# Loading order at the start, one program order over all engines, and a sixth pair tile in a layernorm, attention and SwiGLU block

## The chip, the cores and the metric

The kernel runs on one core of one Trainium2 chip. The metric is the device time of one execution in microseconds (us); the kernel before was run three times, with 853.94, 855.61 and 853.15 us, so its median is 853.94. A profile is one more execution, with a time and a trace of its own.

## The reference

A transformer block with two residual branches, on 2048 rows of 640 columns in fp32. The attention looks at eight earlier positions, two apart; the feed-forward part is a SwiGLU with 1728 hidden columns.

```python
def _A_ref(x, wqkv, wo):                      # H = 32 heads of Dh = 20
    W, dil = 8, 2
    q, k, v = (x @ wqkv).reshape(B, S, 3, H, Dh).transpose(2, 0, 3, 1, 4)
    idx = pos[:, None] - (arange(W) * dil)[None, :]
    mask = idx >= 0
    logits = einsum("bhsd,bhswd->bhsw", q, k[idx]) * Dh ** -0.5
    attn = softmax(where(mask, logits, -1e9))
    return einsum("bhsw,bhswd->bhsd", attn, v[idx]) @ wo      # heads side by side
def _B_ref(x, w_gate, w_up, w_down):          # F = 1728
    return (silu(x @ w_gate) * (x @ w_up)) @ w_down

h  = x + _A_ref(_layernorm(x), wqkv, wo)
h2 = h + _B_ref(_layernorm(h), w_gate, w_up, w_down)
```

## The kernel before

**Tiling.** The 2048 rows are four blocks of 512 (`NB`), and a block is four rows of 128 partitions (`NJ`; "row j" below means such a group of 128, with 640 columns). The 640 inner columns are five chunks of 128 (`NC`). Every fp32 product is made of three passes over high and low parts: `hi` is the value rounded by ACT's copy to the matmul type fp32r, `lo` the rest, made by a subtraction; the passes are hi by hi, lo by hi and hi by lo. So each operand goes through a cast (ACT, mostly) and a subtraction (DVE, mostly) before PE can use it. `low` at L300 issues that subtraction.

**Stages.** For each block `ln1` (L465) normalises x and puts its transpose into `sha` or `shb`; `qkv` (L528) multiplies it by the weights in four column groups (`NG`, 480, 480, 512 and 448 columns, matmuls at L551) and `evict` (L556 to L558, ACT) takes the results from the banks to a stage, from which they go to scratch in device memory (`ksc`, `vsc`, `qsc`). Attention fetches them from there shifted by the window and works mostly on DVE, in `pq`: the product with the keys (L622) and its sum (L628), the product with the values (L663) and the halving sums (L672), a transpose (L679). `wo` multiplies the result by wo (L756). The feed-forward part `ffn` (L918) goes through 14 tiles of the hidden columns (`NF`; 13 of 128 and a last one of 64). A tile of the ordinary kind is `classic` (L898): `load_ffn` fetches and splits its weights, `proj` (matmuls at L844) makes the gate in bank 5 and the up projection in bank 6, `gate_up` takes the SiLU on ACT (L882), multiplies on DVE (L883, which also frees bank 6) and splits the result (L873, L875, L877), and `down` (L859) adds its share to banks 0 to 4. The low parts of the weights, made in block 0, are kept in device memory in `lsc` and read back (L830) for blocks 1 and 2. All 16 groups of attention work and the feed-forward parts of blocks 0 and 1 run interleaved, DVE on the one while PE is on the other.

**Blocks 2 and 3** share weights in `pair` (L1159). Its first `EARLY` tiles (tiles 0 to 7) are done for block 2 by `classic` and once more for block 3. Tiles 8 to 12 go through `pair_tile` (L966): sums and differences of the two blocks' inputs (`sums`, L931) and of the weights are multiplied by `mult` (L1005, matmuls at L1012), and DVE adds the products together, in the manner of a fast matrix product. It yields the hidden columns of both blocks; block 3's wait in `psc` in device memory until `kept_tile` (L1049) fetches them. `finish` adds the residual (DVE, L1203) and stores.

**The start.** `load_x` (L436, its DMA at L441) fetches row j of block 0 by itself, 320 KB. `load_wqkv` (L504) fetches the first column group in parts of chunks ("fifths", 240 KB each; L515), casts each on ACT (L522) and subtracts on DVE (L523). The first fifth goes out on ACT's DMA queue, all the rest on SP's. `ln1` in block 0 takes rows 0 and 1 with `one_dve` (L360: statistics L367, centring L369) and rows 2 and 3 with `one` (L338: mean and centring on ACT, L345, L346 and L350, and the sum of squares on ACT, L357). A row's five chunks are transposed on PE (L495), four into bank 7 (rows 0, 2) or bank 6 (rows 1, 3) and one into its quarter of bank 5, copied by ACT (L497: the high part) and subtracted by DVE (L498). Before that PE runs ten matmuls on zeros, and an eleventh between rows 0 and 1 (`warm`, L419 to L422). The projection's scaling by 1/sqrt(var) is left to `evict`.

**What sets the order.** Each instruction or small group is an entry of a `Plan` (L133) with its engine, a cost and a priority; `add` finds its dependencies by overlapping memory. `order` (L155) takes from the table `ORDER`, per engine, the sequence of that engine's entries, and makes one program of the five sequences: it goes round the engines and takes from each as many entries as have their dependencies issued. Each engine executes its own entries strictly in that sequence. Where a tile or bank is written by several entries, what a reader waits for also depends on where it stands in the program: it waits for the newest write to that tile that stands ahead of it.

Of the kernel before, what the change touches and what calls it, by code (L numbers as in the profile page):

```python
# [25 lines left out]
EARLY = 8  # L26
# [12 lines left out]
ORDER = {  # L39
# [93 lines left out]
class Plan:  # L133
# [21 lines left out]
    def order(self):  # L155
        mine, queue = {}, {}
        for n, o in enumerate(self.ops):
            mine.setdefault(o[0], []).append(n)
# [34 lines left out]
def program(tc, x_in, wqkv_in, wo_in, ffn_in, ffl_in, const_in, out):  # L193
    nc = tc.nc
    V, A, T, Q, G = nc.vector, nc.scalar, nc.tensor, nc.sync, nc.gpsimd
    P = Plan()
# [5 lines left out]
    with tc.tile_pool(name="sb", bufs=1) as sb, tc.tile_pool(  # L202
# [73 lines left out]
        def f(o, n):  # L276
            return fa[:, o : o + n]
# [1041 lines left out]
```

## Time and profile before

| what | value |
|---|---|
| median of three runs (lowest, highest) | 853.94 us (853.15, 855.61) |
| the profiled execution, its own time | 854.99 us |
| its span, first to last instruction | 853.3 us |
| PE matmul / weight load | 843.5 / 717.0 us busy |
| DVE / ACT / POOL | 689.4 / 418.7 / 3.3 us busy |
| DMA | 177.75 MB, mean 208 GB/s |
| PE's granted clock, mean | 1.0 |

PE is TensorE, PEld its weight loads, which run beside the matmuls; DVE is VectorE, ACT ScalarE, POOL GpSimd, SP SyncE, which issues most DMAs here. L551 is line 551 of the kernel. A group like `L844 PE MATMUL bank<-shb,ra` is all instructions of a line with the same operands; the number in brackets behind a row, or the column "idle before", is the time the engine stood still ahead of it and what it then waited for. DMA rows name the target, the source and the queue that issued it. The engines' busy times overlap, and the share of one says only how much of the span it was at work.

### The profile page before, as it was taken

How to read it: one execution, taken by the hardware profiler on the slowest of the kernel's cores; microseconds unless marked ns; L12 is line 12 of the kernel's file. 1: busy time of each engine (PE TensorE's matmuls, PEld its weight loads, DVE VectorE, ACT ScalarE, POOL GpSimd, SP SyncE). 2: the span in 40 equal slices, each digit the busy share in tenths (PEclk: the TensorE clock that was granted, in tenths of full speed). 3: DMA queues.
4: the chain of work that ended last, by engine and by line, in shares of the span. 5: the costliest groups of instructions: out<-in, count | busy, mean ns of one | idle time of the engine just before them, and what ended most of it. 6: DMA issues, size and time to landing. Idle time of an engine off the chain costs nothing.

```text
span 853.3 us, 10728 instructions
## 1 busy us (share of the span) xinstructions
PE 843.5 (99%) x3977; PEld 717.0 (84%) x3977; DVE 689.4 (81%) x807; ACT 418.7 (49%) x736; POOL 3.3 (0%) x12
## 2 busy tenths in 40 slices
PE   8999999999999999999999999999999999999998
PEld 6888888889988888888887898888888888888886
DVE  5499999999999999989989999997766976452433
ACT  5877385252773435367534458444456333242321
POOL 0000000000000000000000000000000000000000
PEclk9999999999999999999999999999999999999999
DMA  6898797688598898657998986967663233244312
GB/s 218 272 287 203 233 257 196 158 259 213 166 263 277 260 284 268 223 191 229 309 302 243 300 241 224 334 224 276 232 201 93 65 127 87 76 167 142 108 39 84
DMA packets 86852, 177.75 MB, mean 208 GB/s; under 512 B 33408, under 2 KB 51584, under 8 KB 86032
## 3 DMA queue, kind: packets, MB, share of 16 engines
q1 hardware_dynamic: 85248, 176.17, 67.7%
q10 hardware_dynamic: 1552, 0.90, 0.4%
q8 instruction: 31, 0.51, 0.3%
q14 instruction: 21, 0.17, 0.1%
HBM read 132.07 MB, written 43.65 MB: 206 GB/s over the span
## 4 chain that ended last, share of the span: by engine, by line
PE 90%; DMA 5%; DVE 4%; SPq 0%; issue 0%; ACT 0%; DVEq 0%
PE bank L844 30%; PE bank L551 24%; PE bank L859 19%; PE bank L1012 7%; PE bank L756 6%; PE bank L1089 2%; DMA ra<-lsc 2%; DMA fa<-in_ffn_dram 2%; DVE pq L663 1%; PE bank L407 1%; DMA pq<-qsc 1%; DVE pq L672 1%; DVE pq L628 1%; DMA fa<-in_x_dram 0%; DVE h L1203 0%
## 5 line engine op out<-in xcount | busy, mean ns | idle before, releaser
L844 PE MATMUL bank<-shb,ra 128*128 128x512 f32 x1050 | 252.7, 390 | 2.0 <-DVE fa L883 1.2
L844 PEld LDWEIGHTS bank<-shb,ra 128*128 128x128 f32 x1050 | 196.0, 188 | 42.5 <-DVE fa L883 1.7
L859 PE MATMUL bank<-ra,acts 128*128 128x512 f32 x656 | 167.2, 390 | 0.0
L859 PEld LDWEIGHTS bank<-ra,acts 128*128 128x128 f32 x656 | 122.4, 188 | 24.7
L551 PE MATMUL bank<-ra,sha 128*128 128x512 f32 (+2 forms) x480 | 107.5, 381 | 0.6 <-ACT sha L497 0.4
L551 PE MATMUL bank<-ra,shb 128*128 128x512 f32 (+1 forms) x470 | 102.5, 378 | 0.0
L551 PEld LDWEIGHTS bank<-ra,sha 128*128 128x128 f32 x480 | 89.1, 188 | 14.3 <-ACT sha L497 0.6
L551 PEld LDWEIGHTS bank<-ra,shb 128*128 128x128 f32 x470 | 88.1, 188 | 12.9
L622 DVE TENSOR_TENSOR pq<-kv,pq 128x2560 f32<-128x2560 f32 x32 | 90.3, 2822 | 3.6 <-issue 2.1
L663 DVE TENSOR_TENSOR pq<-kv,pq 128x2560 f32<-128x2560 f32 x32 | 90.4, 2824 | 2.3 <-DMA kv<-vsc 1.5
L672 DVE TENSOR_TENSOR pq<-pq 128x1280 f32<-128x1280 f32 (+2 forms) x96 | 89.6, 933 | 2.1
L628 DVE TENSOR_REDUCE pq<-pq 128x128 f32<-128x2560 f32 x32 | 90.1, 2816 | 0.3
L558 ACT ACTIVATE st<-bank,fa 128x480 f32<-128x480 f32 (+3 forms) x120 | 50.8, 472 | 74.2 <-PE bank L551 68.7
L820 DVE TENSOR_TENSOR ra<-fa,ra 128x640 fp32r<-128x640 f32 (+1 forms) x70 | 56.2, 819 | 17.4 <-ACT ra L810 13.5
L825 ACT CAST ra<-fa 128x1280 fp32r<-128x1280 f32 (+1 forms) x41 | 50.2, 1224 | 40.1 <-DMA fa<-in_ffn_dram 24.1
L873 ACT CAST acts<-fa 128x512 fp32r<-128x512 f32 x52 | 32.3, 620 | 70.0 <-DVE fa L883 58.7
L810 ACT CAST ra<-fa 128x640 fp32r<-128x640 f32 x56 | 40.7, 728 | 51.2 <-PE bank L859 44.1
L883 DVE TENSOR_TENSOR fa<-bank,fa 128x512 f32<-128x512 f32 x42 | 28.9, 687 | 40.4 <-PE bank L844 40.2
L882 ACT ACTIVATE fa<-bank 128x512 f32<-128x512 f32 x42 | 25.1, 598 | 68.2 <-PE bank L844 60.7
L756 PE MATMUL bank<-ra 128*128 128x320 f32 x360 | 55.7, 309 | 0.0
L756 PEld LDWEIGHTS bank<-ra 128*128 128x128 f32 x360 | 54.1, 188 | 1.5 <-ACT fa L759 0.3
L859 PE MATMUL bank<-acts,ra 128*128 128x512 f32 x164 | 45.8, 390 | 0.0
(163 smaller groups left out, 872.0 us busy)
## 6 DMA issues: line engine op xcount, KB each, us to landing
fa<-in_ffn_dram SPq DMA_DIRECT2D x47, 960.0 KB, 6.0
kv<-ksc SPq DMA_DIRECT2D x32, 440.0 KB, 6.7
kv<-vsc SPq DMA_DIRECT2D x32, 440.0 KB, 6.9
ra<-lsc SPq DMA_DIRECT2D x21, 640.0 KB, 6.2
lsc<-ra SPq DMA_DIRECT2D x13, 640.0 KB, 4.9
ra<-lsc SPq DMA_DIRECT2D x23, 320.0 KB, 5.0
ksc<-st SPq DMA_DIRECT2D x32, 160.0 KB, 4.4
pq<-qsc SPq DMA_DIRECT2D x16, 320.0 KB, 5.2
```

The costliest lines, as they stand in the source:

```text
L551: T.matmul(banks[bk][:, 0:n], l, r_(wq(g, w, c) + shift, n), start=(p, c) == first_mm, stop=(p, c) == last_mm)
L558: P.add("ACT", act(m) + 0.06, lambda: A.activation(stage_t()[:, o : o + NJ * m].rearrange("p (t j c) -> p t j c", j=NJ, c=w)[:, :, j, :], ...
L622: P.add("DVE", dve(2560), lambda: V.tensor_tensor(pq(PROD, 2560).rearrange("p (j w c) -> p j w c", j=2, w=W), window(ko, 2 * jp), pq(qo + ...
L628: P.add("DVE", dve(2560), lambda: V.tensor_reduce(logits(lo)[:, :, 16 * jp : 16 * jp + 16].rearrange("p h n -> p n h"), pq(PROD, 2560).rea ...
L663: V.tensor_tensor(pq(PROD, 2560).rearrange("p (j n d) -> p j n d", j=2, d=DH), bass.AP(tensor=v.tensor, offset=v.offset, ap=[list(v.ap[0]) ...
L672: V.tensor_add(dst(v), v[:, :, 0:m, :], v[:, :, m : 2 * m, :])
L756: T.matmul(banks[bk][:, 0:320], l, r_(m, 320), start=p == 0 and c == 0, stop=p == 2 and c == NC - 1)
L820: low(640, lambda E, o=o: E.tensor_sub(ws(t, lo + o, 640)[p0:], fa[p0:, raw + o : raw + o + 640], ws(t, hi + o, 640)[p0:].bitcast(F32)), [ ...
L825: P.add("ACT", act(n), lambda: A.copy(ws(wt, gu, n), f(raw, n)), r=[rf(raw, n)], w=[rws(wt, gu, n)], prio=PR["fh"])
L844: T.matmul(banks[bk], ws(wt, gu + 1280 * w + wid * c + col, 128), x(a, c), start=p == 0 and c == 0, stop=p == 2 and c == NC - 1)
L859: T.matmul(banks[k], l, m, start=first and p == 0, stop=stop and p == len(passes) - 1)
L1012: T.matmul(banks[bk], ws(wt, o + 2048 * w + 128 * k, 128), xv_[k](a), start=first and p == 0 and k == 0, stop=stop and p == 2 and k == n - ...
```

## The change

Four things change; no arithmetic outside of them does.

1. `EARLY` falls from 8 to 7: tile 7 of blocks 2 and 3 goes through `pair_tile` and `kept_tile`, so that there are six pair tiles.
2. At the start each fifth of the first weight group is a DMA of its own, and the first one moves from ACT's queue to SP's. The calls now alternate: row 0, fifth 0, row 1, fifths 1 and 2, row 2, fifths 3 and 4, row 3.
3. `ORDER` is one table over all engines, of triples (engine, index, count), and `order` issues the program exactly in that sequence instead of merging five.
4. The table's content is new for every engine. The factors on the planner's bytes for the first transfers (1.45 before) are 1.3, and 1.1 for row 0 of x; `order` does not read them.

```diff
-EARLY = 8
+EARLY = 7
...
-ORDER = {
-    "PE": (
-        0, 2, 1, 3, 5, 4, (10, 6), (25, 2), 16, (27, 5), (6, 2), (32, 2), (17, 6), 34, 23, (35, 7), 24, (42, 8), 8, (50, 3), 9, (53, 15), 70, (68, 2), 73, 72,
...
+    (1, 594, 1), (0, 766, 1), (1, 595, 1), (0, 771, 1), (1, 597, 1), (2, 728, 1), (0, 773, 1), (1, 596, 1), (2, 729, 1), (0, 775, 1), (2, 730, 1), (0, 772, 1),
...
     def order(self):
-        mine, queue = {}, {}
+        mine = {e: [] for e in ENGINES}
         for n, o in enumerate(self.ops):
-            mine.setdefault(o[0], []).append(n)
-        for e, runs in ORDER.items():
-            queue[e] = [mine[e][i] for r in runs for i in (range(r[0], r[0] + r[1]) if isinstance(r, tuple) else (r,))]
-            assert sorted(queue[e]) == mine[e]
-        done, out, at = set(), [], dict.fromkeys(queue, 0)
-        while len(out) < len(self.ops):
-            before = len(out)
-            for e, q in queue.items():
-                while at[e] < len(q) and self.ops[q[at[e]]][3] <= done:
-                    done.add(q[at[e]])
-                    out.append(q[at[e]])
-                    at[e] += 1
-            assert len(out) > before
+            mine[o[0]].append(n)
+        out, done = [], set()
+        for e, i, c in ORDER:
+            for n in mine[ENGINES[e]][i : i + c]:
+                assert self.ops[n][3] <= done
+                done.add(n)
+                out.append(n)
+        assert len(done) == len(self.ops)
         return out
...
-                P.add("SP", 0.45, lambda j=j: Q.dma_start(f(XR + 640 * j, 640), x_in[0, :, j, :]), w=[rf(XR + 640 * j, 640)], prio=0, nbytes=1.45 * nb(128, 2560))
+                P.add("SP", 0.45, lambda j=j: Q.dma_start(f(XR + 640 * j, 640), x_in[0, :, j, :]), w=[rf(XR + 640 * j, 640)], prio=0, nbytes=(1.3 if j else 1.1) * nb(128, 2560))
...
-                    first = g == 0 and ks[0] == 0
-                    P.add("ACT" if first else "SP", 0.45, lambda: (A if first else Q).dma_start(f(o, n).rearrange("p (k c) -> p k c", c=m)[:, :, o0:o1], wqkv_in[h, :, ks[0] : ks[-1] + 1, lo : lo + o1 - o0]),
+                    P.add("SP", 0.45, lambda: Q.dma_start(f(o, n).rearrange("p (k c) -> p k c", c=m)[:, :, o0:o1], wqkv_in[h, :, ks[0] : ks[-1] + 1, lo : lo + o1 - o0]),
...
         load_wqkv(0, ((0,),))
-        load_wqkv(0, ((1, 2),))
         load_x(0, (1,))
-        load_wqkv(0, ((3, 4),))
-        load_x(0, (2, 3))
+        load_wqkv(0, ((1,), (2,)))
+        load_x(0, (2,))
+        load_wqkv(0, ((3,), (4,)))
+        load_x(0, (3,))
```

The calls set the numbering of the entries; the sequence on SP is the table's. All line numbers rise by 117 or 118: L441 becomes L559, L497 becomes L615, L551 becomes L668, L844 becomes L961, L883 becomes L1000, L1012 becomes L1129.

SP's sequence at the start, before. A row gives the line, what it does, the tile written and read (`fa` is the fp32 work tile, `in_x_dram` and `in_wqkv_dram` the inputs) and its shape; x2 stands for two in a row. A transfer of 128x480 is one fifth, of 128x960 two.

```order
L441 DMA fa_65<-in_x_dram 128x640 x2
L515 DMA fa_65<-in_wqkv_dram 128x960
L441 DMA fa_65<-in_x_dram 128x640
L515 DMA fa_65<-in_wqkv_dram 128x960 x2
L441 DMA fa_65<-in_x_dram 128x640
L515 DMA fa_65<-in_wqkv_dram 128x960
```

The rows are 0 and 1, then 2, then 3; the third transfer of weights is already one of the second column group. The same place in the changed kernel:

```order
L559 DMA fa_65<-in_x_dram 128x640 x3
L632 DMA fa_65<-in_wqkv_dram 128x480 x3
L559 DMA fa_65<-in_x_dram 128x640
L632 DMA fa_65<-in_wqkv_dram 128x480 x2
L632 DMA fa_65<-in_wqkv_dram 128x960 x2
L632 DMA fa_65<-in_wqkv_dram 128x480
L556 DMA fa_65<-in_x_dram 128x2560
```

The first three are now rows 0, 2 and 1, ahead of any weight; the five fifths follow, row 3 among them, and then the second group; block 1 of x (L556) comes before the third.

ACT's sequence at the start, before (`sha` takes the transposed rows' high parts, `ra` the weights' high parts):

```order
L515 DMA fa_65<-in_wqkv_dram 128x480
L310 ACT_TABLE_LOAD
L310 ACTIVATE fa_65<-fa_65 128x1
L522 CAST ra_66<-fa_65 128x480
L497 CAST sha_131<-bank5_74 128x128
L497 CAST sha_131<-bank7_76 128x512
L497 CAST sha_131<-bank5_74 128x128
L522 CAST ra_66<-fa_65 128x480 x2
L497 CAST sha_131<-bank6_75 128x512
L345 ACTIVATE fa_65<-fa_65 128x640
L346 ACTIVATE fa_65<-fa_65 128x1
L350 ACTIVATE fa_65<-fa_65 128x640
```

and after:

```order
L428 ACT_TABLE_LOAD
L428 ACTIVATE fa_65<-fa_65 128x1
L463 ACTIVATE fa_65<-fa_65 128x640
L464 ACTIVATE fa_65<-fa_65 128x1
L468 ACTIVATE fa_65<-fa_65 128x640
L615 CAST sha_129<-bank7_76 128x512
L475 ACTIVATE fa_65<-fa_65 128x640
L639 CAST ra_66<-fa_65 128x480 x2
L615 CAST sha_129<-bank6_75 128x512
L615 CAST sha_129<-bank7_76 128x512
L639 CAST ra_66<-fa_65 128x480
```

Row 2's centring (L463, L464, L468) now stands first, then the copy of row 0 from bank 7, row 2's squares (L475), two fifths, and the copies of rows 1 and 2 from banks 6 and 7. In the program ahead of the copy from bank 7 stand only row 0's transposes.

In the middle of the program the place on DVE of the multiplication that frees bank 6 is shown by a stretch of block 0's feed-forward part, before (L663 and L672 are attention, L820 the low parts of weights, L883 the multiplication, L875 the low part of its result):

```order
L663 TENSOR_TENSOR pq_87<-kv_68,pq_87 128x2560
L820 TENSOR_TENSOR ra_66<-fa_65,ra_66 128x640 x2
L883 TENSOR_TENSOR fa_65<-bank6_75,fa_65 128x512
L672 TENSOR_TENSOR pq_87<-pq_87 128x2x640
L875 TENSOR_TENSOR acts_2056<-fa_65,acts_2056 128x512
L672 TENSOR_TENSOR pq_87<-pq_87 128x2x320
L672 TENSOR_TENSOR pq_87<-pq_87 128x2x160
L679 STREAM_TRANSPOSE pq_87<-pq_87 128x2x5x32
```

and after:

```order
L780 TENSOR_TENSOR pq_88<-kv_68,pq_88 128x2560
L1000 TENSOR_TENSOR fa_65<-bank6_75,fa_65 128x512
L937 TENSOR_TENSOR ra_66<-fa_65,ra_66 128x640 x2
L992 TENSOR_TENSOR acts_2087<-fa_65,acts_2087 128x512
L789 TENSOR_TENSOR pq_88<-pq_88 128x2x640
L937 TENSOR_TENSOR ra_66<-fa_65,ra_66 128x640
L789 TENSOR_TENSOR pq_88<-pq_88 128x2x320
L789 TENSOR_TENSOR pq_88<-pq_88 128x2x160
L796 STREAM_TRANSPOSE pq_88<-pq_88 128x2x5x32
```

Here L1000 now stands right behind the multiply of 2560 columns, ahead of the two weight subtractions that it followed before. Over the whole program 9 of the 42 such operations stood right behind one of 2560 columns before, and 14 of 41 do after.

More of the change, by code (lines that the diff above doesn't have):

```diff
@@ L36 @@
 PR = {'x': 0.4, 'wqd': 10, 'wqh': 10, 'wql': 10, 'qev': 6, 'kvs': 6, 'atl': 10, 'exp': 2.2, 'ost': 1, 'wod': 6, 'woh': 8, 'wol': 0.5, 'old': 6, 'fld': 4, 'lst': 10, 'wev': 3, 'fh': 1.2, 'fl': 0.4, 'ln1': 10, 't1': 1.5, 'wo0': 4, 'wo': 6}
-ORDER = {
[24 rows of a table removed]
-    ),
-    "ACT": (
[19 rows of a table removed]
-    ),
-    "DVE": (
[20 rows of a table removed]
-    ),
-    "POOL": (
-        (0, 17), 34, (17, 6), 35, (23, 11), (36, 3),
-    ),
[18 rows of a table removed]
-    ),
-}
+ENGINES = ("PE", "ACT", "DVE", "POOL", "SP")
+ORDER = (
[212 rows of a table added]
+)
 class Plan:
@@ L513, in ld @@
                 def ld(h, o0, o1, lo, ks=ks, o=o, n=n):
-                    first = g == 0 and ks[0] == 0
-                    P.add("ACT" if first else "SP", 0.45, lambda: (A if first else Q).dma_start(f(o, n).rearrange("p (k c) -> p k c", c=m)[:, :, o0:o1], wqkv_in[h, :, ks[0] : ks[-1] + 1, lo : lo + o1 - o0]),
-                          w=[rf(o + m * i + o0, o1 - o0) for i in range(len(ks))], prio=PR["wqd"] * (g > 0), nbytes=nb(128 * len(ks), 4 * (o1 - o0)) * (1.0 if g else 1.45))
+                    P.add("SP", 0.45, lambda: Q.dma_start(f(o, n).rearrange("p (k c) -> p k c", c=m)[:, :, o0:o1], wqkv_in[h, :, ks[0] : ks[-1] + 1, lo : lo + o1 - o0]),
+                          w=[rf(o + m * i + o0, o1 - o0) for i in range(len(ks))], prio=PR["wqd"] * (g > 0), nbytes=nb(128 * len(ks), 4 * (o1 - o0)) * (1.0 if g else 1.3))
                 ld(g, 0, min(m, 480), c0)
```

290 rows, old and new, of the table ORDER are left out of this document.

## The prediction

> **What bounds the kernel now.** I began with the first part of the page and the sum over its chain of waits.
>
> ```profile
> span 853.3 us, 10728 instructions
> PE 843.5 (99%) x3977; PEld 717.0 (84%) x3977; DVE 689.4 (81%) x807; ACT 418.7 (49%) x736; POOL 3.3 (0%) x12
> ```
>
> PE is busy for 843.5 of 853.3 us, so 9.8 us are idle. A table of stretches shows where they lie (the first columns are the stretch, its length, then busy time and count of PE, PEld, DVE, ACT, POOL).
>
> ```profile
> 0.00:10.00 10.00, 6.18 (x22) 4.26 (x22) 5.27 (x12) 3.31 (x7) 1.18 (x7) 1.00 0.81 294
> 400.00:500.00 100.00, 98.05 (x454) 81.81 (x453) 93.31 (x88) 42.86 (x62) 0.00 (x0) 1.00 0.97 289
> 660.00:745.00 85.00, 85.00 (x377) 70.38 (x376) 58.36 (x87) 28.50 (x44) 1.36 (x3) 1.00 0.27 89
> 840.00:853.30 13.30, 9.46 (x44) 7.49 (x42) 4.88 (x8) 1.32 (x3) 0.00 (x0) 1.00 0.25 99
> ```
>
> The first ten microseconds hold 3.8 us of idle PE, the end 3.8, the stage from 400 to 500 some 1.95; the pair stage (660 to 745) none. The waits of PE name who was late in the first three that count.
>
> ```profile
> PE bank L495 <- DVE fa L369: 2.0, 2, 1.5
> PE bank L422 <- POOL ra L1220: 1.4, 1, 1.4
> PE bank L844 <- DVE fa L883: 1.2, 1, 1.2
> PE bank L844 <- DMA ra<-lsc: 0.7, 1, 0.7
> ```
>
> So a change pays here in three ways only: fewer matmuls, useful matmuls sooner at the start, or fewer stalls in the middle. ACT and DVE have room of their own and count only where PE waits for them.
>
> **The sixth pair tile.** Tile 7 of the feed-forward part leaves the ordinary scheme, in which blocks 2 and 3 take 2 projections of 3 passes over 5 chunks each, 60 matmuls of 512 columns, and enters `pair_tile`, whose calls of `mult` make 7 x 6 + 4 x 3 = 54. The chain of waits has a long unbroken piece of that line.
>
> ```profile
> 661.62 14.28 PE bank L1012 x63
> ```
>
> That is 0.2267 us each, and six fewer save 6 x 0.2267 = 1.36 us of PE. The tile's extra sums and differences fall on DVE and ACT and its intermediate goes out to `psc` and back. The stretch from 660 to 745 above has five such tiles with DVE busy 58.4 of 85 us, ACT 28.5 and the DMA share at 0.27, and no idle PE; a sixth of the same density hides as well. If that cover were gone, each operation would cost its length, but a third of DVE's time is free, so I count nothing.
>
> **The start.** These rows of the timeline carry it (start, length, engine, line, operation, and in brackets the idle time before it).
>
> ```profile
> 0.81 0.86 SPq L441 DMA_DIRECT2D fa<-in_x_dram  x2
> 0.81 0.41 ACTq L515 DMA_DIRECT2D fa<-in_wqkv_dram  x1
> 5.00 0.89 DVE L367 BATCH_NORM_STATS2 fa<-fa 128x6 f32<-128x320 f32 x2 [2.86 <-DMA fa<-in_x_dram]
> 6.17 0.55 DVE L369 TENSOR_SCALAR fa<-fa 128x640 f32<-128x640 f32 x1
> 6.87 0.74 PE L495 MATMUL bank<-fa 128*128 128x128 f32 x5 [1.46 <-DVE fa L369]
> 7.80 0.55 DVE L369 TENSOR_SCALAR fa<-fa 128x640 f32<-128x640 f32 x1
> 8.40 0.77 PE L495 MATMUL bank<-fa 128*128 128x128 f32 x5 [0.56 <-DVE fa L369]
> 8.77 0.92 ACT L497 CAST sha<-bank 128x128 fp32r<-128x128 f32 x3 [3.01 <-PE bank L495]
> 9.57 0.49 PE L551 MATMUL bank<-ra,sha 128*128 128x480 f32 x1 [0.41 <-ACT sha L497]
> 10.55 0.61 ACT L497 CAST sha<-bank 128x512 fp32r<-128x512 f32 x1
> 11.03 0.77 ACT L345 ACTIVATE fa<-fa 128x640 f32<-128x640 f32 x1
> 12.89 1.07 ACT L522 CAST ra<-fa 128x480 fp32r<-128x480 f32 x2
> 22.12 0.75 ACT L357 ACTIVATE fa<-fa 128x640 f32<-128x640 f32 x1
> 22.85 0.73 ACT L357 ACTIVATE fa<-fa 128x640 f32<-128x640 f32 x1
> ```
>
> Row 0 of x is there at 5.0 us. Its four transposes end near 7.5, yet ACT's first copy of it starts only at 8.77, right after the second group of transposes at 8.40 began: the copy from bank 5 stands first in ACT's order and waits for the newest write to that bank, which is row 1's. So rows 0 and 1 both have to be through before one matmul of the projection runs, at 9.57. Two parts of the change act here. The row of x no longer shares the DMA engines with the first fifth of the weights, and the new program order lets ACT copy row 0's wide part when row 0's own transposes are done.
>
> When does row 0 land? The answers of the DMA view, first for the transfers of 0.81 us, then for one that ran alone at 10.90, and the rate in steps of half a microsecond from zero:
>
> ```profile
> fa<-in_x_dram SPq DMA_DIRECT2D x1, 320.0 KB, 4.2
> fa<-in_wqkv_dram ACTq DMA_DIRECT2D x1, 240.0 KB, 4.3
> fa<-in_wqkv_dram SPq DMA_DIRECT2D x1, 480.0 KB, 3.5
> GB/s 0 0 0 46 79 163 250 393 423 416 417 415 410 420 425 422 415 422 392 382 169 5 0 61 131 215 401 222 104 215 245 56 0 0 54 84 73 326 392 158
> ```
>
> The late bound is no gain: 0.81 + 4.2 = 5.0. The early bound takes the lone transfer: 3.5 us for 480 KB, less 160 KB at about 417 GB/s (0.4), is 3.1, so 3.9. Without the 246 thousand bytes of weights beside it, at the rate of these rows, row 0 would be 0.59 sooner, at 4.4. I take 4.5, since most of the wait is the slow climb of the rate, which the change leaves. The Trainium skill ("DMA: Bandwidth & Descriptors", section "Queues, rings and completion order") says that each DMA engine takes turns between the queues that have work; by that rule half of the turns go back to row 0 and the gain is the whole 0.59, the sum below 0.1 better. The trace agrees so far: 320 KB on one queue and 240 KB on the other landed 0.1 us apart.
>
> On SP the order is now rows 0, 2, 1, three single fifths, row 3, two fifths. At 417 GB/s a row takes 0.79 us and a fifth 0.59, so row 2 lands at 5.3, row 1 at 6.1, the first fifth at 6.7 (before: 5.1), the last near 9.9. From there ACT alone sets the pace. By the rows above, centring a row takes it 11.03 to 12.89 = 1.86 us, the sum of squares 22.12 to 22.85 = 0.73, a copy of 512 columns 0.48 until the next may start and 0.61 until done, a fifth 0.5 and 0.57. In its new order: row 2 centred 5.3 to 7.2; row 0 copied 7.2 (its transposes end near 6.9: 4.5 + 1.72 on DVE + 0.7); squares 7.7 to 8.4; first fifth done 9.0; second 9.5; row 1 copied by 10.0; row 2 by 10.5; third fifth by 11.0; row 3 centred 10.9 to 12.8; fourth fifth by 13.3. The first matmul can start at about 9.1, behind row 2's transposes. Now the matmuls, against these pieces of the chain:
>
> ```profile
> 10.23 3.12 PE bank L551 x13
> 13.35 0.55 PE bank L495 x5
> 13.90 5.62 PE bank L551 x26
> 19.96 0.65 PE bank L551 x3
> 20.73 16.73 PE bank L551 x77
> ```
>
> Before, at 20.73 us all 20 transposes and 1 + 13 + 26 + 3 = 43 matmuls were done, and from there PE never waits. A matmul takes 5.62 / 26 = 0.216. After: nine of the first 18 are done when the third fifth is there at 11.0, nine more take 1.95 (13.0), row 3's transposes 0.55 (13.6), and 25 more 5.4, so the same point is reached at 19.0, 1.7 us sooner. With row 0 at 5.0 it is 1.2, at 3.9 it is 2.3, if DVE's and ACT's copies keep up as in the rows; a slip of half a microsecond in that chain brings the low end to 0.7. I take 1.6. The first fifth of the weights costs nothing by being 1.6 us later, since ACT reaches it at 8.4; the splitting adds two issues on SP at 0.43 (0.86 / 2 above), under transfers already queued.
>
> **The middle and the end.** All queues have new orders. The two stalls of the middle (1.24 and 0.71) come from places that move: DVE's L883, which frees the bank for the up projection, stood behind a multiply of 2560 columns, and a stored weight landed late. The groups of the page give that multiply's length.
>
> ```profile
> L663 DVE TENSOR_TENSOR pq<-kv,pq 128x2560 f32<-128x2560 f32 x32 | 90.4, 2824 | 2.3 <-DMA kv<-vsc 1.5
> ```
>
> By the order, 9 of the 42 such operations before stand right behind one of DVE's 2560-wide operations, and 14 of 41 after. At one stall of 1.24 in nine that is 0.7 us more; the two old stalls may go (1.95 less) or recur. I take the middle as unchanged, with 1.95 less and 1.5 more as the ends of the likely case. The mask and the halo rows are loaded later, block 1 of x earlier, behind a PE that has 77 matmuls queued: nothing. The end keeps its form (last matmul, one DVE sum, one store): nothing.
>
> Sum: 1.36 + 1.6 = 2.96 us. The profiled execution took 854.99 us with a span of 853.3; the median of the runs is 853.94, 1.05 below it. Taken off the median: 851.0 us.
>
> **The rivals.** A measurement of this kernel can tell about 0.3% from no change, that is 2.56 us: below 851.4 is faster, above 856.5 slower.
>
> The middle improves too: both stalls go, 851.0 - 1.95 = 849.1. For it speaks that every queue is ordered anew; against it, that more of the bank-freeing operations stand behind long ones.
>
> The start gives nothing: ACT now does a row's centring and squares (1.86 + 0.73) ahead of its first weight, and if row 0 lands at 5.0 and the copies slip by another microsecond, the first matmul is at 10.6 instead of 9.57, made up by the third row's transposes being done; only the pair tile is left, 853.94 - 1.36 = 852.6. This is also the case in which the change doesn't do what its words say: by the order three rows go ahead of the weights, not one.
>
> PE's clock falls back at the start. The ten warming matmuls took 4.02 us where ten at 0.2267 take 2.27:
>
> ```profile
> 1.39 4.02 PE L422 MATMUL bank<-ra 128*128 128x512 f32 x10 [1.39 <-POOL ra L1220]
> ```
>
> If PE dropped to that again at its gaps after 5.4 us, another 1.75 would be lost: 852.8. Against it: before, gaps of 1.46, 0.56 and 0.41 were followed by 13 matmuls at 0.24 each, and the new gaps are shorter (0.9, then under half a microsecond). The Trainium skill ("TensorE: Matmul & The Clock Gate", section "Part 1: The HAM clock gate (the "warmup" mystery)") has the rule: an idle window of about 3.4 us halves the clock, and the window runs freely. By it a sparse start can be caught; the trace has no such case, its granted clock is 1.00 in every stretch.
>
> Slower than before: DVE becomes the wait in the middle, where the stretch from 400 to 500 us above has it busy 93.3 of 100. PE's next up projection waits for L1000 (L883 before), and L1000 for the 2.82 us ahead of it. At the 1.24 us of the one stall seen, five of the fourteen places give 6.2, 857.2 us; it decides from an extra loss of 5.5. Against it: eight of the nine places before cost nothing, since a down projection covers them.
>
> **How the numbers follow.** The forecast has 0.55; both stalls gone 0.13; an empty start 0.18; the clock 0.05; DVE in the middle 0.09. Of the forecast's case, whose own spread is about 1 us either way round 851.0, seven parts in ten lie below 851.4: 0.55 x 0.7 + 0.13 = 0.51 faster; 0.165 + 0.18 + 0.05 = 0.40 the same; 0.09 slower. The range runs from the case without stalls, 849.0, to the empty start with 1 us more of stalls, 853.6; left out are the slow case and about 1 in 10 beyond the ends.
>
> **What would show it.** Right: DVE's first statistics start near 4.5, ACT's first copy near 7.2, PE's first projection matmul near 9.1, and 43 of them with all transposes done by 19.0; six matmuls fewer; PE idle in the first ten microseconds still near 3 us, in the middle about 2. Wrong: row 0 at 5.0, a first matmul after 9.6, matmuls at 0.4 us behind 9 us, or PE's waits for L1000 over 4 us in total.

## The result

The changed kernel takes 850.97 us (median of 20 runs, 849.79 to 854.62). The kernel before, run in turn with it, takes 855.6 (20 runs, 852.82 to 860.1). The ratio is 0.9946, 95% interval 0.9931 to 0.9961: faster, by 4.6 us, half a per cent. The time was forecast at 851.0 and came out there. The drop was forecast at 2.96, from a median of three runs (853.94) that lay below that of twenty. So two things need explaining: 4.6 us instead of 3, and why the kernel before spreads over 7 us.

The profiled execution of the changed kernel took 850.46 us. The first part of its page:

```profile
span 848.7 us, 10718 instructions
PE 841.7 (99%) x3971; PEld 716.4 (84%) x3971; DVE 694.1 (82%) x815; ACT 420.7 (50%) x738; POOL 2.6 (0%) x11
```

Six matmuls fewer, as counted. PE is idle for 7.0 us instead of 9.8. The stretches that lost time before:

```profile
0.00:10.00 10.00, 7.02 (x28) 5.47 (x29) 5.66 (x13) 6.36 (x13) 1.16 (x7) 1.00 0.81 277
400.00:500.00 100.00, 100.00 (x462) 83.87 (x461) 96.40 (x89) 44.09 (x62) 0.00 (x0) 1.00 0.97 299
840.00:848.70 8.70, 4.85 (x24) 3.68 (x22) 3.43 (x6) 0.00 (x0) 0.00 (x0) 1.00 0.39 151
```

The end is unchanged (3.85 idle). The stretch from 400 to 500, which lost 1.95, loses nothing, although DVE is busier there (96.4 of 100). PE's waits confirm it. All that the view names, with their total, count and longest:

```profile
PE bank L613 <- DVE fa L487: 1.6, 1, 1.6
PE bank L540 <- POOL ra L1337: 1.4, 1, 1.4
```

No L1000 and no stored weights (`lsc`) are left. The start, in rows of the timeline:

```profile
3.86 0.89 DVE L485 BATCH_NORM_STATS2 fa<-fa 128x6 f32<-128x320 f32 x2 [1.74 <-DMA fa<-in_x_dram]
4.62 0.74 ACT L463 ACTIVATE fa<-fa 128x640 f32<-128x640 f32 x1 [2.33 <-DMA fa<-in_x_dram]
6.53 0.59 ACT L615 CAST sha<-bank 128x512 fp32r<-128x512 f32 x1
6.77 0.89 DVE L485 BATCH_NORM_STATS2 fa<-fa 128x6 f32<-128x320 f32 x2 [1.19 <-DMA fa<-in_x_dram]
8.54 1.25 PE L613 MATMUL bank<-fa 128*128 128x128 f32 x9 [1.60 <-DVE fa L487]
9.56 4.16 PE L668 MATMUL bank<-ra,sha 128*128 128x480 f32 x18
```

Row 0 is there at 3.9 us (before 5.0) and ACT copies it at 6.5 (before 8.8). Yet the first projection matmul stands at 9.56, as before: row 1 went out third, landed at 6.7, and its transposes stand ahead of that matmul. What is gained shows behind it. Two pieces of the chain of waits:

```profile
9.80 3.91 PE bank L668 x18
13.71 0.55 PE bank L613 x5
14.26 18.72 PE bank L668 x87
```

At 14.26 all transposes and 18 matmuls are done, and from there a matmul takes 18.72 / 87 = 0.215. The 43rd is through at 14.26 + 25 x 0.215 = 19.6, before at 20.73: 1.1 us. For the two profiled executions that makes 1.36 (pair tile) + 1.1 (start) + 1.95 (waits of the middle) = 4.4 of the 4.6 between the spans.

### The profile page after: what moved, and what is told of

It is laid out like the page before. It is cut to its first block, busy times and chain, and to the rows that moved or that the text cites. A ratio compares the mean times of both kernels' runs of the same rounds, so it can differ in the third digit from the quotient of the medians.

```text
span 848.7 us, 10718 instructions
## 1 busy us (share of the span) xinstructions
PE 841.7 (99%) x3971; PEld 716.4 (84%) x3971; DVE 694.1 (82%) x815; ACT 420.7 (50%) x738; POOL 2.6 (0%) x11
## 4 chain that ended last, share of the span: by engine, by line
PE 97%; DVE 1%; DMA 1%; ACTq 0%; issue 0%; SPq 0%; ACT 0%
PE bank L961 33%; PE bank L668 24%; PE bank L976 22%; PE bank L1129 9%; PE bank L873 6%; PE bank L1206 2%; PE bank L525 1%; DMA fa<-in_x_dram 1%; ACTq L1272 0%; PE bank L613 0%; PE bank L1313 0%; DVE fa L1246 0%; DVE fa L485 0%; SPq L559 0%; DVE fa L1260 0%
## 5 line engine op out<-in xcount | busy, mean ns | idle before, releaser
L961 PE MATMUL bank<-shb,ra 128*128 128x512 f32 x1035 | 248.0, 390 | 0.1
L961 PEld LDWEIGHTS bank<-shb,ra 128*128 128x128 f32 x1035 | 193.1, 188 | 39.7 <-ACT fa L999 0.9
L668 PE MATMUL bank<-ra,sha 128*128 128x512 f32 (+2 forms) x480 | 105.6, 379 | 0.0
L668 PE MATMUL bank<-ra,shb 128*128 128x512 f32 (+1 forms) x470 | 102.6, 378 | 0.0
L668 PEld LDWEIGHTS bank<-ra,sha 128*128 128x128 f32 x480 | 89.5, 188 | 12.8
L668 PEld LDWEIGHTS bank<-ra,shb 128*128 128x128 f32 x470 | 88.0, 188 | 12.6
L937 DVE TENSOR_TENSOR ra<-fa,ra 128x640 fp32r<-128x640 f32 x69 | 55.0, 819 | 17.1 <-ACT ra L927 15.3
L1000 DVE TENSOR_TENSOR fa<-bank,fa 128x512 f32<-128x512 f32 x40 | 27.5, 688 | 43.4 <-PE bank L961 29.4
```

What stands on the lines that cost most here:

```text
L668: T.matmul(banks[bk][:, 0:n], l, r_(wq(g, w, c) + shift, n), start=(p, c) == first_mm, stop=(p, c) == last_mm)
L937: low(640, lambda E, o=o: E.tensor_sub(ws(t, lo + o, 640)[p0:], fa[p0:, raw + o : raw + o + 640], ws(t, hi + o, 640)[p0:].bitcast(F32)), [ ...
L961: T.matmul(banks[bk], ws(wt, gu + 1280 * w + wid * c + col, 128), x(a, c), start=p == 0 and c == 0, stop=p == 2 and c == NC - 1)
```

## The experiments

Every kernel below computes the whole reference. Names with b are edits of the kernel before, with a of the changed one. Each has one trace, that of its first run. "Row 0" is the start of DVE's first statistics there, when row 0 of x has landed (5.00 us in the kernel before, 3.86 in the changed one); the "48th" is the start of the 48th projection matmul, with all transposes and nothing but the start ahead of it (21.45 before, 20.40 after).

| run | n | lowest, median, highest us | ratio to before, interval | row 0 | 48th |
|---|---|---|---|---|---|
| b_two_moves | 12 | 852.31, 852.82, 854.80 | 0.9960 (0.9939 to 0.9980) | 4.63 | 21.05 |
| b_lsc | 12 | 852.49, 853.34, 855.51 | 0.9979 (0.9965 to 0.9993) | 4.70 | 21.13 |
| b_copy2 | 12 | 851.81, 852.21, 854.26 | 0.9958 (0.9935 to 0.9980) | 5.09 | 21.59 |
| b_start | 12 | 850.52, 853.61, 858.24 | 0.9969 (0.9945 to 0.9992) | 3.94 | 19.88 |
| b_start2 | 12 | 850.51, 851.23, 855.06 | 0.9955 (0.9929 to 0.9981) | 3.76 | 19.88 |
| a_pair5 | 12 | 851.46, 853.44, 857.07 | 0.9966 (0.9943 to 0.9989) | 3.89 | 20.08 |
| a_merge | 12 | 850.56, 852.19, 857.39 | 0.9963 (0.9939 to 0.9988) | 3.80 | 20.46 |
| a_late | 12 | 851.08, 855.47, 863.49 | 0.9999 (0.9972 to 1.0025) | 3.77 | 19.58 |
| a_lsc | 6 | 849.59, 849.85, 850.22 | 0.9939 (0.9920 to 0.9958) | 3.82 | 19.74 |
| a_rows | 12 | 851.22, 853.74, 857.00 | 0.9979 (0.9962 to 0.9996) | 4.05 | 20.77 |
| a_w0_act2 | 12 | 850.34, 850.77, 851.69 | 0.9939 (0.9912 to 0.9966) | 5.00 | 20.60 |
| a_best | 12 | 849.57, 849.91, 851.63 | 0.9923 (0.9899 to 0.9948) | 3.88 | 19.74 |

The kernel before, beside them on three chips, had medians of 855.31, 856.54 and 856.13, from 852.2 to 862.4. That spread makes the intervals wide, so most of what follows compares kernels whose own runs lie close together; their medians come from different chips and are not paired. The chips themselves differ little: the lowest run of the kernel before is 852.20, 852.29 and 852.20 on them. The ratios in the table are those on record; they are not quotients of these medians.

The 99 runs of the kernel before on these chips fall into two groups by the mean granted clock that is on record for each. In 48 it is 0.998 or less, and their median is 857.5 us; in 51 it is 0.999 or 1.000, and their median is 853.9. Every run above 857.7 is of the first group. A stretch of 3.4 us at half clock, as b_start below has one, lowers the mean to 0.998. So in about half of its runs PE's clock seems to fall once or more.

**b_two_moves.** The two stalls of the middle, undone where they stood.

```diff
+MOVES = (("DVE", 496, 282), ("SP", 429, 280))
 ORDER = {
...
+            for w, i, j in MOVES:
+                if w == e:
+                    queue[e].remove(mine[e][i])
+                    queue[e].insert(queue[e].index(mine[e][j]), mine[e][i])
             assert sorted(queue[e]) == mine[e]
```

> The kernel before, with two entries moved in its table: on DVE the multiplication of block 1's tile 5 that frees bank 6 (L883) goes ahead of the 2560-column multiply it stood behind, and on SP the load of tile 8's stored low weights goes ahead of one load of values for the attention. Theory A (the gain after is a sum of three: start 1.0, sixth pair tile 1.4, the two stalls in the middle some 2.0 us): PE's waits for L883 (1.24) and for the stored weights (0.71) are gone, nothing takes their place, and the time falls by 2.0 to 2.5 us, to a ratio of 0.9971 to 0.9977. Theory B (these stalls are chance of one execution, or PE just waits a little later): a ratio within 0.001 of 1.

Both waits are gone, the median is 2.5 us under the 855.31 beside it, and the highest of 12 runs is 854.8 where before went to 862.4. Theory A was right on the places; that the spread goes too spoke for B's word "chance". The load of the stored weights, on SP's queue, in the trace of before and then of this run:

```profile
471.93 0.43 SPq L830 DMA_DIRECT2D ra<-lsc  x1
```

```profile
469.14 0.32 SPq L835 DMA_DIRECT2D ra<-lsc  x1
```

The view of the tile `lsc` for that one load gives its landing, with the same numbers in both:

```profile
DMA to landing us min/median/max: 11.6/11.6/11.6
```

In before PE wanted it at 482.9 (0.71 ahead of 483.62): 11.0 us after the issue. Any delay is a stall. The moved load lands at 469.14 + 11.6 = 480.7, and PE comes to it near 480.8, five matmuls behind 479.75, so it has almost no room either; b_copy2, with the same move, waits for it in its trace:

```profile
PE bank L849 <- DMA ra<-lsc: 0.3, 1, 0.3
```

**b_start.** The changed kernel's code with eight ordinary tiles, its order up to the 44th projection matmul, before's from there.

```diff
-EARLY = 7
+EARLY = 8
```

> The kernel before with the changed kernel's start alone: its transfers and its sequences on all engines up to the 44th matmul of the projection, then everything in the order of before, with eight ordinary tiles. Theory A: the first projection matmul at 9.6 us, the 48th at 20.4 instead of 21.4, both stalls of the middle still there, and the time 1.0 us lower, a ratio near 0.9988. Rival, the start's 1.6 us as forecast: a ratio near 0.9981. Theory B (the gain at the start shifts transfers against DVE and is lost in the middle): 1.000, with other or longer stalls.

The start came out as theory A had it or better (48th at 19.9). The ratio, 0.9969, cannot tell 1.0 from 1.6 us here, for the middle is before's, and in this profiled execution it was bad. PE's rows around tile 8, then two of its four waits:

```profile
480.02 1.29 PE L928 MATMUL bank<-shb,ra 128*128 128x512 f32 x5
485.24 5.14 PE L928 MATMUL bank<-shb,ra 128*128 128x512 f32 x15 [3.92 <-DMA ra<-lsc]
```

```profile
PE bank L928 <- DMA ra<-lsc: 3.9, 1, 3.9
PE bank L928 <- DVE fa L967: 1.2, 1, 1.2
```

The same load, issued at 471.21, was used at 485.24, 14.0 us later. And the wait cost more than itself. Stretches of half a microsecond; the first 1.00 or 0.50 behind POOL's column is the granted clock:

```profile
484.50:485.00 0.50, 0.00 (x0) 0.00 (x0) 0.00 (x0) 0.00 (x0) 0.00 (x0) 0.94 1.14 283
485.00:485.50 0.50, 0.26 (x1) 0.26 (x2) 0.00 (x0) 0.00 (x0) 0.00 (x0) 0.50 1.15 272
487.50:488.00 0.50, 0.50 (x3) 0.36 (x2) 0.19 (x1) 0.22 (x1) 0.00 (x0) 0.50 1.00 391
488.50:489.00 0.50, 0.50 (x4) 0.41 (x3) 0.50 (x1) 0.00 (x0) 0.00 (x0) 1.00 0.98 400
```

PE's clock fell to half at the end of a gap of 3.92 us and stayed there until near 488.4 (the slice from 488.0 has 0.64), with two or three matmuls begun in a slice instead of four. PE worked from 485.24, so some 3.1 us went at half speed, about 1.6 us lost by estimate. The Trainium skill ("TensorE: Matmul & The Clock Gate", section "Part 1: The HAM clock gate (the "warmup" mystery)") has it: an idle window of about 3.4 us halves the clock, and it comes back after a busy one. The trace agrees, with 3.92 idle and some 3.4 at half. In a_late below, gaps of 2.56 and 0.93 left it at 1.00. The mean clock of this run is 0.998. That the slower half of the runs of the kernel before had such a gap as well is likely but not shown, since there is no trace of them.

**b_lsc.** SP's move alone.

```diff
-MOVES = (("DVE", 496, 282), ("SP", 429, 280))
+MOVES = (("SP", 429, 280),)
```

> The kernel before with one entry moved on SP alone: tile 8's stored low weights of block 1 are loaded ahead of the attention's values instead of behind them, some 2.8 us earlier; the multiplication L883 stays behind the 2560-column multiply. Theory D (the kernel before varies from 852 to 862 us because this load lands about when PE wants it, and a long wait also drops PE's clock): the runs lie close together, within some 3 us, as with both moves (852.3 to 854.8), their median is about 1.2 us above that of both moves, near 854.0, and PE waits for L883 alone. Theory E (DVE's multiplication is the cause of the spread): the runs spread as before, over 6 us or more.

The runs lie within 3.0 us (852.49 to 855.51, where the kernel before went from 852.29 to 859.44 beside them), as theory D said, so this load is most of what spread them. The median is 0.5, not 1.2, above that of both moves. In its profiled execution PE did not wait for L883's counterpart: DVE began the multiply ahead of it at 458.0 instead of 460.5. In the kernel before DVE had stood still earlier (2.1 us for nothing that the profile shows, 0.8 for keys), and here it had not. So L883's stall, 1.24 us in before and 1.2 in b_start, is a matter of chance as well.

**a_lsc.** The same idea on the changed kernel: SP's entries 414 (tile 3's low weights), 423 (tile 6) and 432 (tile 8) some places earlier.

```diff
 SP:
-... 258, 257, 419, 414 ... 265, 266, 270, 264, 423 ... 283, 432 ...
+... 414, 258, 257, 419 ... 423, 265, 266, 270, 264 ... 432, 283 ...
```

> The changed kernel with three loads of stored low weights in block 1 (tiles 3, 6 and 8) a few places earlier on SP, ahead of the attention loads and stores they stood behind. Theory D: the changed kernel too has runs in which such a load is late (849.8 to 854.6 in 20 runs); with more room the runs lie within 2 us and the median falls by 0.5 to 1 us, to about 850.2, a ratio to before of 0.994. Rival (the spread of the changed kernel has another cause, or the attention loads that are pushed back now make DVE late): median 851 or more, spread 4 us or more.

All 6 runs lie within 0.63 us, at 849.85: the rival is out, and no other version spreads less or has a lower median. Two later kernels with the same three moves lie within 1.35 us (a_w0_act2) and 2.06 us (a_best) in 12 runs. PE waits only at the start:

```profile
PE bank L543 <- POOL ra L1340: 1.4, 1, 1.4
PE bank L616 <- DVE fa L490: 1.0, 1, 1.0
```

**a_late.** Tile 8's load late on SP.

```diff
 SP:
-... 283, 432, 433, 437, 284, 435, 401, 400, 399, 436 ...
+... 283, 433, 437, 284, 435, 401, 400, 399, 432, 436 ...
```

> The changed kernel with the same load (tile 8's stored low weights, block 1) issued some 9 us later on SP, behind a load of values and three loads of attention results; nothing else moves. Theory D: PE waits there 4 to 5 us for it, the granted clock falls behind the wait for about 3 us, which costs another 1.5, and every run rises by 5 to 7 us, to 856 to 858, above the kernel before. Without a fall of the clock the rise is the wait alone, 4 to 5 us. Rival (the load is early enough in the changed kernel, with 13 us from issue to need, that the delay is absorbed by the transfers around it): under 2 us.

The median rose by 4.5 us over 850.97, but not by the way expected: the lowest run is 851.08, the highest 863.49. In the profiled execution the late load cost 0.93; two other waits cost more. The rows of the loads, and the third wait:

```profile
423.69 1.43 PE L964 MATMUL bank<-shb,ra 128*128 128x512 f32 x5 [2.56 <-DMA ra<-lsc]
489.94 1.42 PE L964 MATMUL bank<-shb,ra 128*128 128x512 f32 x5 [0.93 <-DMA ra<-lsc]
```

```profile
PE bank L671 <- ACT st L678: 2.1, 1, 2.1
```

The first is tile 3's load, which this kernel issues as the changed one does. The last stands at 69.38 us: a load of x, issued at 48.18, landed 15.1 us later (10.8 in the changed kernel), ACT stood still 4.92 us for it, and the copy that PE waited for came behind. So another load than those of the stored weights can be late too; a_rows has the same wait of PE with 1.4 us, and a_best moves this load. The load made late went out at 484.74, 13.6 us later than in the changed kernel, and landed in 5.2; in the changed kernel it took 7.3. So theory D's sum, a fixed stall of 4 to 5 us, was wrong. The profiled execution kept its clock at 1.00. Seven of the other 11 runs have a mean clock of 0.994 to 0.998, the longest (863.49) 0.994; where they waited is not known, as there is no trace of them.

**a_merge.** The changed kernel's sequences through before's merge in `order`.

```diff
-        for e, i, c in ORDER:
-            for n in mine[ENGINES[e]][i : i + c]:
-                assert self.ops[n][3] <= done
-                done.add(n)
-                out.append(n)
+        queue = {e: [] for e in ENGINES}
+        for e, i, c in ORDER:
+            queue[ENGINES[e]] += mine[ENGINES[e]][i : i + c]
+        done, out, at = set(), [], dict.fromkeys(queue, 0)
...
```

> The changed kernel with the same sequence on each engine, but merged into one program engine by engine as before, instead of in the order of the one table. Theory A (what counts is each engine's own sequence): the same time as the changed kernel, a ratio to before of 0.9946, within 0.001. Theory C (the one program order is what removes waits, since a reader waits for the newest write to a tile that stands ahead of it in the program): waits like the one of ACT's first copy come back, at the start and in the feed-forward part, and the time rises by 0.5 us or more.

Open. The median is 1.2 above the changed kernel's, but the intervals of the two ratios overlap. Its trace has one wait that the changed kernel lacks, and once more tile 3's load:

```profile
14.02 0.33 PE L618 MATMUL bank<-fa 128*128 128x128 f32 x1 [0.59 <-DVE sha L621]
419.46 1.43 PE L966 MATMUL bank<-shb,ra 128*128 128x512 f32 x5 [0.17 <-DMA ra<-lsc]
```

The 0.59 is of theory C's kind: a transpose into a quarter of bank 5 waits for DVE's subtraction (L621), by our reading because it reads other quarters and now stands ahead of it in the program. So the one order is worth at most 0.6 us at the start, and the 48th shows none of it (20.46, against 20.40 in the changed kernel); more is not shown.

**a_pair5.** The changed kernel with one pair tile less.

```diff
-EARLY = 7
+EARLY = 8
```

> The changed kernel with five pair tiles instead of six: its order up to tile 7 of block 2, then the sequence of before, shifted, with a few entries around the seam moved. Theory A: six more matmuls of 0.2267 us, so 1.36 us over the changed kernel if the seam costs nothing, a ratio to before near 0.996; PE's waits tell what the seam adds (each of its microseconds is to be taken off). Rival (the sixth pair tile also costs something on DVE, so that leaving it out gives part of it back): less than 1 us over the changed kernel.

Its lowest run is 1.67 above the changed kernel's lowest. In the profiled execution the seam, where the two orders meet, costs 0.50:

```profile
631.83 1.43 PE L963 MATMUL bank<-shb,ra 128*128 128x512 f32 x5 [0.50 <-DVE fa L1002]
```

The profiled spans differ by 1.5 (850.2 and 848.7). Without the 0.50, and with the 0.32 by which this start came sooner (48th at 20.08 and 20.40), 1.3 is left for the pair tile, near 1.36; the medians (853.44 against 850.97) are blurred by the loads in the middle.

**b_start2.** b_start with both moves of the middle; in its numbering of SP's entries the load is 432.

```diff
-... DVE 282, 496 ... SP 283, 432 ...
+... DVE 496, 282 ... SP 432, 283 ...
```

> The kernel before with both moves of the middle (L883 ahead of the long multiply, tile 8's stored weights earlier) and the changed kernel's start; eight ordinary tiles. Both moves alone gave 852.8 us with little spread. Theory A with the start at the size that the traces show (the 48th projection matmul at 20.0 us on average, before 21.2): 1.2 us less, 851.6, within 0.4. The forecast's term: 1.6 less, 851.2. What is left from here to the changed kernel with its loads moved (849.85) is then the pair tile, 1.36 by the count.

851.23: 1.59 below b_two_moves, and a_lsc is 1.38 below this. Those are near the two terms of the forecast, 1.6 and 1.36, but theory A's 851.6 within 0.4 holds this median as well. By lowest runs the steps are 1.80 and 0.92, and by the 48th this start gains 1.2 (21.05 to 19.88). Neither step is pure: this kernel also has the one program order throughout, and a_lsc another order in the middle. The only wait of PE that the view names is that for the zeros of the warming:

```profile
PE bank L507 <- POOL ra L1304: 1.4, 1, 1.4
```

**b_copy2.** Both moves, and the copy from bank 7 ahead of that from bank 5.

```diff
-MOVES = (("DVE", 496, 282), ("SP", 429, 280))
+MOVES = (("DVE", 496, 282), ("SP", 429, 280), ("ACT", 7, 8))
```

> The kernel before with both moves of the middle and ACT's copy of row 0 from bank 7 ahead of its copy from bank 5; nothing else of the start changes. Theory A (the wait for row 1 by ACT's first copy costs something at the start): that copy starts near 7.3 us instead of 8.8, the first projection matmul behind row 1's transposes near 9.2, and the time falls by 0.2 to 0.5 us from 852.8. Rival (PE has to pass row 1's transposes anyway, so the copy's wait is covered): the same time within 0.1, and the wait of PE for that copy (0.4) replaced by one for weights.

0.61 below b_two_moves in the median, 0.50 in the lowest. The trace doesn't show how: in its execution row 0 landed late (5.09), and the copy, behind row 0's transposes, started at 8.29. Counted from row 0, ACT's first copy is 0.57 sooner than in b_two_moves (3.20 and 3.77 behind it), but the 48th is not: it stands 16.50 behind row 0, and 16.42 to 16.45 in the three traces with the copy in its old place. The time is that of theory A; the trace is that of the rival, that the copy's wait is covered. This stays open.

**a_w0_act2.** a_lsc with the first fifth on ACT's queue again.

```diff
-                    P.add("SP", 0.45, lambda: Q.dma_start(...
+                    first = g == 0 and ks[0] == 0
+                    P.add("ACT" if first else "SP", 0.45, lambda: (A if first else Q).dma_start(...
...
```

> The changed kernel with its three loads moved, and with the first fifth of the weights on ACT's queue again, issued beside row 0 as before. Theory of the forecast (row 0 alone lands 0.6 us sooner): row 0 lands about 0.6 later, DVE's first statistics start at 4.4 to 4.9 instead of 3.9, and the time rises by 0.3 to 0.6 over 849.85. Rival (the first matmul waits for row 1, which lands third, and the bytes ahead of that row are what counts): row 1 lands as much later as row 0, and the first projection matmul comes 0.3 to 0.6 later, with the same rise. If row 0 is later and the time the same, what row 0 gains by being alone is worth nothing here.

0.92 above a_lsc, more than any side expected, and no run of one lies among those of the other. DVE's first statistics and PE's first projection matmul, in a_lsc and then in this run:

```profile
3.82 0.89 DVE L488 BATCH_NORM_STATS2 fa<-fa 128x6 f32<-128x320 f32 x2 [1.70 <-DMA fa<-in_x_dram]
...
8.93 4.14 PE L671 MATMUL bank<-ra,sha 128*128 128x480 f32 x18
```

```profile
5.00 0.89 DVE L488 BATCH_NORM_STATS2 fa<-fa 128x6 f32<-128x320 f32 x2 [2.88 <-DMA fa<-in_x_dram]
...
9.47 4.45 PE L672 MATMUL bank<-ra,sha 128*128 128x480 f32 x18
```

Beside the weights row 0 lands at 5.0, as in the kernel before; first on the one queue, at 3.8. In this pair 240 KB beside it cost it 1.2 us, twice their 0.59 at the full rate. Over all traces it is less: the five with a fifth beside row 0 have it at 4.63 to 5.09, the nine without at 3.76 to 4.05, so 1.0 on average. The start pays 0.86 of it (48th 20.60 against 19.74). It comes by way of DVE: row 1's statistics, which here stand right behind row 0's without a wait for data, start at 6.67 instead of 6.14, and the first projection matmul is 0.54 later.

**a_rows and a_best.** SP loads rows 0 and 1 first; ACT casts two fifths, and copies rows 0 and 1, ahead of centring row 2; PE multiplies ahead of row 1's transposes. a_best adds the moves of a_lsc, puts row 2's and row 3's transposes sooner on PE, and issues block 1's x ahead of two loads of wo. The start of a_rows:

```diff
 SP:
-row 0, row 2, row 1, fifths 0, 1, 2, row 3, fifths 3, 4
+row 0, row 1, fifths 0, 1, 2, 3, row 2, fifth 4, row 3
 ACT:
-centre 2, copy 0, squares 2, cast 0, 1, copy 1, 2, cast 2, centre 3, cast 3
+cast 0, copy 0, cast 1, copy 1, cast 2, 3, centre 2, copy 2, cast 4
```

> The changed kernel with another start: SP loads rows 0 and 1, four fifths, row 2, the last fifth, row 3; ACT casts the first two fifths ahead of centring row 2; PE multiplies row 0 by the first fifth ahead of row 1's transposes; from the 60th projection matmul on the order is the changed kernel's. Theory F (in the changed kernel PE's first matmul waits for row 1, which lands third, and for ACT's centring of row 2): the first projection matmul comes near 7.5 us instead of 9.6, the 48th at 19.0 to 19.6 instead of 20.4, and the time falls by 0.8 to 1.4 us. Rival (ACT is the limit from then on, so that a sooner first matmul only waits for later rows): PE waits for ACT between 10 and 16 us for as much as it gained, and the time stays.

> The changed kernel with its three loads moved, the start of the run with rows 0 and 1 first, row 2's transposes now four matmuls sooner and row 3's eight sooner, so that they no longer stand behind work that waits for them, and block 1's x issued ahead of two loads of wo. Theory F mended: the first projection matmul near 7.3 us, the 18th at 12.0, no wait for ACT behind it, the 48th at 19.4 (19.8 with the loads moved alone), and 0.3 to 0.5 us less than 849.85. Rival (ACT is the limit): the 48th at 19.8 or later and no gain.

The first projection matmul moves to 7.2 and 7.05, and nothing comes of it. PE in a_rows, then in a_best:

```profile
7.22 0.49 PE L669 MATMUL bank<-ra,sha 128*128 128x480 f32 x1 [0.33 <-ACT sha L616]
13.97 3.81 PE L669 MATMUL bank<-ra,sha 128*128 128x480 f32 x15 [0.57 <-ACT sha L616]
```

```profile
7.05 0.49 PE L670 MATMUL bank<-ra,sha 128*128 128x480 f32 x1 [0.33 <-ACT sha L617]
7.84 3.97 PE L670 MATMUL bank<-ra,sha 128*128 128x480 f32 x15
```

In a_best the 48th stands at 19.74, as in a_lsc, and the median is 849.91 against 849.85. The first matmul comes 1.9 us sooner than in a_lsc (8.93), and two things use that up. A row's transposes take PE about 0.46 us, and two more rows of them stand behind the first matmul here, 0.9 together. The rest, about 1.0 by difference, are matmuls that come late: 15 take 3.97 us here, 0.26 each, where 18 in a_lsc take 4.14, 0.23 each. PE's weight loads between 7 and 20 us wait 0.8 for DVE's low parts of x, 0.6 for ACT's copies and 0.3 for DVE's low parts of the weights. So the rival held in its result, but ACT is not the limit alone: PE has the same transposes to do, and DVE's parts come late more often than ACT's. a_rows, 2.8 above the changed kernel in the median, had other waits in its trace: 2.3 for tile 3's load, and the 1.4 behind the load of x.

## Why the prediction was right, and where not

- **The sixth pair tile, 1.36.** Right: six matmuls fewer, no wait in the pair stage. From the 48th projection matmul to the end of the span, less PE's waits, the traces with five pair tiles take 829.5 to 830.2 us (six, without b_start and its fallen clock) and those with six 828.2 to 828.6 (five; a_late and a_rows, with waits over 2 us, have 829.4): 1.4. The medians of b_start2 and a_lsc differ by 1.38, their lowest runs by 0.92.
- **The start, 1.6.** About right in size. The medians of b_two_moves and b_start2 differ by 1.59. The traces show less: 1.1 in the pair of profiled executions, and 1.3 on average over all (the 48th at 21.05 to 21.59 in four with the start of before, at 19.58 to 20.46 in seven with the changed one).
- **The steps of the start** were partly wrong. "I take 4.5" for row 0 failed: it lands at 3.8 to 3.9, the early bound, because 0.59 for the bytes beside it was too little; they cost 1.0 on average. The Trainium skill's rule of engines that take turns between queues ("DMA: Bandwidth & Descriptors", section "Queues, rings and completion order") was weighed there as giving the whole 0.59. The traces went beyond both. This landing accounts for about 1.0 of the 1.3: the 48th stands 16.4 to 16.5 behind row 0 with the start of before and 15.8 to 16.7 with the changed one, which leaves 0.3 on average for the new places of copies and casts. "From there ACT alone sets the pace" failed: the first matmul waits for row 1 through DVE (L613, 1.6), and behind it, from 9.80 to 13.71, 18 matmuls run at 0.217 each, PE's own pace. Forecast for that matmul was 9.1; in the seven traces it comes at 8.5 to 9.6.
- **"I take the middle as unchanged."** This is the term that failed. The kernel before loses there, over its quieter version b_two_moves, 855.6 - 852.82 = 2.8 us in the median; the changed one, over a_lsc, 850.97 - 849.85 = 1.1. The change gives back 1.7, where nothing was counted. (That 1.7, 1.59 and 1.38 add up to the measured 4.63 is no test: they are steps between the same medians. The tests are the traces above and, for the middle, the 1.95 us of waits that the profile before has and the one after lacks.) I read 1.24 and 0.71 as fixed costs of two places; they are one draw from transfers and DVE work with no room. In the changed kernel tile 8's load had 13.0 us from issue (471.1) to need (484.1), before 11.0.
- **The rivals.** "Both stalls go" is what the profiled execution shows, and it had the drop nearly right: 2.96 + 1.95 = 4.9, against 4.6 measured. DVE as the wait behind L1000 didn't come: 14 places instead of 9, no wait in the changed kernel's trace, one of 0.50 in a_pair5, at its seam. PE's clock did not fall at the start; it fell in the middle, behind 3.9 us without work.
- **Why the time still fitted.** By luck. The base of three runs was 1.7 below the median of twenty, and the drop 1.7 larger than forecast, and the two errors cancel. The base happened to lie 1.1 above the quieter version (853.94 - 852.82), which is what the changed kernel still loses in its middle. Both errors come from the spread of the kernel before: it was in the profile as two waits, and I took it for constant.

## What to carry to other kernels

When a kernel's runs spread by a per cent, look for a load that lands just when it is wanted: compare each load's time from issue to need with its time to landing, and move the tight ones ahead of transfers that have room. Here that was three entries of one queue, for 1.1 us and most of the spread (4.8 us in 20 runs before, 0.6 in 6 after). A wait in one profile is one draw; the granted clock on record for each run tells of the runs without a trace. Here the first transfer was worth having without another queue beside it, and a first matmul that came sooner was worth nothing, since the ones behind it did not come at PE's pace and the same transposes were still to be done.

## What the hardware did that was not expected

- Tile 8's load of 640 KB, among busy transfers (DMA share 0.97 from 400 to 500 us in both kernels), landed 11.6 us after its issue in before and in b_two_moves, b_lsc and b_copy2, 7.3 in the changed kernel, and was used 14.0 after it in b_start.
- A wait of 3.92 us in mid-kernel halved PE's clock for 3.4 us; waits of 2.56 us and less did not. In 48 of 99 runs of the kernel before the mean clock is 0.998 or less, and those are 3.5 us longer in the median.
- The first transfer of the kernel landed 1.0 us sooner on average without 240 KB beside it (1.2 in one pair), though these bytes take 0.59 at the full rate.
